# A second MLP's weights: 64-bit words made into floats early and kept in DRAM

## The chip, the cores and the metric

The kernel runs on one core of a Trainium2 chip. The metric is device time in microseconds (us). The kernel before took 886.29 us (median of 3 runs, 883.88 to 888.55).

## The reference, cut to what matters

Attention over four batches of eight heads of 576 x 64 (a local band plus a four-fold downsampled attention) gives `x`, four batches of 576 x 512. Then a first block with a LayerNorm and an MLP, and a second block with a token MLP and a channel MLP:

```
x  = x + relu(LN(x) * g_ln @ moe_w_ch1) @ moe_w_ch2          # 512 -> 2048 -> 512
h  = relu(x^T @ w_tok1) @ w_tok2                             # over the 576 tokens, 576 -> 256 -> 576
u  = x + h^T
out = u + relu(u @ w_ch1) @ w_ch2                            # 512 -> 1536 -> 512
```

The weights come as 64-bit floats; the attention inputs and the result are 32-bit.

## The kernel before, in words

**Numbers.** A product of 32-bit floats is made of three TensorE passes over a high and a low part (`PASSES`: high by high, high by low, low by high). So each operand exists as `hi` (a rounded copy) and `lo` (the rest). Weights are read as pairs of 32-bit integers. `convert_steps` makes a 32-bit float `f` of each pair with three VectorE operations (exponent, sign, tail; L257, L262, L267), then ScalarE copies `f` to `hi` (L272) and VectorE subtracts to get `lo` (L275). The raw words lie in a staging slot (tag `st`), `f` in a buffer of the tag `cv`, `hi` and `lo` in a weight buffer of the pool `wp`.

**Units and chunks.** The 2304 tokens are 18 tiles of 128, and two tiles make a chunk: nine chunks for each MLP (0 to 8 for the first, 9 to 17 for the second). A unit is 128 of the hidden columns in one chunk. The first MLP has 16 units a chunk (`UA`), the second 12 (`UB`). For unit `i` of the sequence the first product `g1` (L875, 12 matmuls of 256 columns), `relu` on ScalarE (L884), `low` on VectorE (L888) and the second product `g2` (L901, 6 matmuls of 512 columns) follow each other, and `g1` of unit `i + 1` is put before `g2` of unit `i`. The accumulators leave at the end of a chunk (`evac`, L910 and L914). Units 0 to 111 (chunks 0 to 6) stand in a written order together with the attention (`STEPS`). From unit 112 on a loop emits the steps, and `put(position, step)` hangs other work on a unit: `put(131.5, ...)` comes after the second product of unit 131, a whole number before it.

**What sets the order.** A planner takes the emitted steps as priorities and places each instruction on its engine as early as its own simulated times, its inputs and a free buffer allow. Work that was put on unit 113 can so run beside units of a lower number, between the written steps. `keep_in_program_order` pins one instruction behind the one emitted before it on its engine. Each engine then runs its list in order, and all loads and stores are issued by SyncE's queue (SP), in order too.

**The weights.** A unit's weights are two pieces of 512 x 128 words (`NPC` = 2): the first piece is for `g1`, the second for `g2`. `wp` has 16 buffers, and in chunks 7 and 8 all of them hold units of the first MLP. So a unit of the second MLP gets a buffer only when chunk 8 (units 128 to 143) has used a unit for the last time. The token MLP's relu results take buffers of the same pool. When the attention is over, `close_att` opens a new staging pool with two `st` slots and two `cv` buffers; the token weights (`load_tok`, 9 pieces) and the second MLP's 24 pieces use it. `units_b` adds the 24 pieces to a list at unit 129, `w_load` issues as many loads as there are slots, and `w_split` (one call for each unit, from unit 131.5 on, one unit apart) converts two pieces and loads the next ones:

```
    for m in range(UB):
        put(bw + 3.5 + m, w_split, NPC)
```

**Beside it** stand the token steps (`put_tok`): `xs_load` (L968, L970) into one buffer `xr`, `xs_split` (ScalarE L976, GpSimd L977), `tok1` (TensorE L992), `tok_relu`, and for each chunk `u_load` (L1009), `tok2` (L1023, L1028) and the turning of the chunk's tokens (`xt_turn`: 16 transfers of 16 KB for each tile on SP, L818, then L830 and L835).

Of the kernel before, what the change touches and what calls it, by code (L numbers as in the profile page):

```python
# [7 lines left out]
F32 = mybir.dt.float32  # L8
F32R = mybir.dt.float32r
I32 = mybir.dt.int32  # L10
ACTF = mybir.ActivationFunctionType
ALU = mybir.AluOpType
# [4 lines left out]
DM = H * D  # L17
# [19 lines left out]
QW = 512  # L37
# [160 lines left out]
def block_kernel(ctx: ExitStack, tc: tile.TileContext, qk, vw, vh, vg, g_ln, wa, t1, t2, wb, band, near, lv, edge, out):  # L198
    nc = tc.nc
    UA = wa.shape[0]  # L200
    UB = wb.shape[0]
# [3 lines left out]
    dram = ctx.enter_context(tc.tile_pool(name="dram", bufs=1, space=DRAM))  # L205
    wp = ctx.enter_context(tc.tile_pool(name="wp", bufs=UA))
# [7 lines left out]
    att_ctx = ExitStack()  # L214
    at = att_ctx.enter_context(tc.tile_pool(name="at", bufs=1))
    sp_ctx = ExitStack()
    sp = {"pool": sp_ctx.enter_context(tc.tile_pool(name="sp", bufs=1)), "n": 3}

    up_scr = [dram.tile([S, 128], F32, name=f"up_scr{n}") for n in range(B * NP)]
    loc_scr = {n: dram.tile([2 * NTL * QB, 128], F32, name=f"loc_scr{n}") for n in range(NP, B * NP)}  # L220
    x2_scr = [dram.tile([128, CT, DM], F32, name=f"x2_scr{c}") for c in range(NCH)]

    ident = const.tile([128, 128], F32, name="ident")
# [15 lines left out]
    def f32(ap):  # L239
        return ap.bitcast(F32)  # L240
# [3 lines left out]
    wt = {}  # L244

    wa, wb, t1, t2 = (w.bitcast(I32) for w in (wa, wb, t1, t2))

    def stage(n):
        return sp["pool"].tile([128, 2 * QW], I32, tag="st", name="st", bufs=sp["n"])[:, :2 * n]

    def convert_steps(raw, hi, lo, n):
        r = raw.rearrange("p (n t) -> p n t", t=2)
        h, l = r[:, :, 1], r[:, :, 0]
        f = sp["pool"].tile([128, QW], I32, tag="cv", name="cv", bufs=2)[:, :n]

        def exponent():
            return nc.vector.tensor_scalar(  # L257
                out=f, in0=h, scalar1=3, scalar2=0x3FFFFFFF, op0=ALU.logical_shift_left, op1=ALU.bitwise_and
            )

        def sign():
            nc.vector.scalar_tensor_tensor(  # L262
                out=f, in0=h, scalar=-0x40000000, in1=f, op0=ALU.bitwise_and, op1=ALU.bitwise_or
            )

        def tail():
            nc.vector.scalar_tensor_tensor(  # L267
                out=f, in0=l, scalar=29, in1=f, op0=ALU.logical_shift_right, op1=ALU.bitwise_or
            )

        def split_hi():
            nc.scalar.activation(out=hi, in_=f.bitcast(F32), func=ACTF.Copy)  # L272

        def split_lo():
            nc.vector.tensor_tensor(out=lo, in0=f.bitcast(F32), in1=f32(hi), op=ALU.subtract)  # L275

        return [exponent, sign, tail, split_hi, split_lo]

    def convert(raw, hi, lo, n):
        for f in convert_steps(raw, hi, lo, n):  # L280
            f()

    ld_w = {}
    NPC = 2 * DM // QW

    def load_unit(i, part, gate=None):
        w, m = (wa, i) if i < UA else (wb, i - UA)
        if i < EARLY:
            if part == 0:
                t = wp.tile([128, NPC, 2 * QW], I32, tag="w", name="raw")  # L290
                for k in range(NPC):
                    ld_w[i, k] = t[:, k]
            raw = ld_w[i, part]
        else:
            raw = ld_w[i, part] = stage(QW)
        if gate is not None:
            nc.vector.tensor_copy(raw[:, 0:1].bitcast(F32), gate)
        nc.sync.dma_start(out=raw, in_=w[m, part])

    def split_steps(i, part):  # L300
        if part == 0:
            wt[i] = wp.tile([128, 2, 2, DM], F32R, tag="w", name="w")
        t = wt[i]
        e, o = divmod(part * QW, DM)
        return convert_steps(ld_w.pop((i, part)), t[:, e, 0, o:o + QW], t[:, e, 1, o:o + QW], QW)
# [732 lines left out]
    def put(pos, f, *args):  # L1038
        u, half = divmod(int(2 * max(pos, UNITS)), 2)
        u = min(u, NSEQ - 1)  # L1040
        (bg if half else mid)[u].append(lambda: f(*args))
# [24 lines left out]
    pieces = [(i, part) for i in range(UA) for part in range(NPC)]  # L1066
    nl, nsp = [0], [0]

    def w_load(n):
        while n and nl[0] < len(pieces) and nl[0] - nsp[0] < sp["n"]:  # L1070
            load_unit(*pieces[nl[0]])
            nl[0] += 1
            n -= 1
# [103 lines left out]
    def close_att():  # L1177
        vec_ctx.close()
        att_ctx.close()
        sp["n"] = 2  # L1180
        sp["pool"] = ctx.enter_context(tc.tile_pool(name="sp2", bufs=1))
        tok["pool"] = ctx.enter_context(tc.tile_pool(name="tok", bufs=1))

    bt = base[NCH - 2]
    put(base[NCH - 1] - 5, rota.__setitem__, slice(None), ["g"])
    put(bt, close_att)
    for i in range(NTL + 4):
        put(bt + 1 + i, load_tok, i)
    put_tok(0, base[NCH - 1] - 4)
    put_tok(1, base[NCH - 1] + 3)  # L1190

    def units_b():
        pieces.extend((UA + i, part) for i in range(UB) for part in range(NPC))

    bw = base[NCH - 1]
    put(bw + 1, units_b)
    put(bw + 1, lambda: w_load(sp["n"]))
    for m in range(UB):
        put(bw + 3.5 + m, w_split, NPC)
    for c in range(NCH, 2 * NCH):  # L1200
        put_prep2(c, base[c] - 1)
    put_tok(2, base[NCH + 2])
# [133 lines left out]
```

## Time and profile before

| | us |
|---|---|
| median of 3 runs | 886.29 (883.88 to 888.55) |
| the profiled execution | 886.56 |
| its span, first to last instruction | 884.8 |
| TensorE matmuls busy (PE) | 863.8 (98%) |
| TensorE weight loads busy (PEld) | 766.3 (87%) |
| VectorE (DVE) | 518.4 (59%) |
| ScalarE (ACT) | 251.4 (28%) |
| GpSimd (POOL) | 193.6 (22%) |
| SP's transfers, share of the 16 DMA engines | 39.4% |

Times in the trace count from the first instruction of the span. A busy time is the sum of the instructions on that engine. PE's weight loads overlap its matmuls. The chain of waits is followed back from the last instruction to what released it; by engine PE has 66% of it, VectorE 19%, transfers 8%.

### The profile page before, as it was taken

The page shows a single profiled execution, that of the slowest core. Times are in us where ns is not written, and L with a number is a line of the kernel's source. Part 1 is how long each engine was busy: PE and PEld are TensorE (multiplying, and loading weights), DVE is VectorE, ACT ScalarE, POOL GpSimd, SP SyncE. Part 2 cuts the span into 40 slices and gives each one's busy share as a digit, 9 for nine tenths or more (in the row PEclk, how much of TensorE's full clock was granted, in tenths as well). Part 3 has the DMA queues.
Part 4 walks back from the last instruction along what each step waited for, and adds up shares of the span by engine and source line. Part 5 has one row for each costly group of instructions (what it writes and reads, how often), then busy time and mean ns, then how long its engine had stood idle before and what let it go on. Part 6 is the DMA issues. An engine that isn't in the chain of part 4 may idle for free.

```text
span 884.8 us, 16767 instructions
## 1 busy us (share of the span) xinstructions
PE 863.8 (98%) x6418; PEld 766.3 (87%) x6418; DVE 518.4 (59%) x1114; ACT 251.4 (28%) x713; POOL 193.6 (22%) x197
## 2 busy tenths in 40 slices
PE   7999999999999999999999999989999999999998
PEld 6888899887989999989999887879898898999997
DVE  5999999999998776832222779863213232222221
ACT  5665535354322111322111233222121111111111
POOL 7731323566873510111000000110010000000000
PEclk9999999999999999999999999999999999999999
DMA  9747776578662522532111356632222121121100
GB/s 280 193 151 225 225 237 199 148 199 224 168 150 72 139 49 60 175 92 89 36 37 48 107 155 178 193 115 53 52 56 46 29 67 35 17 45 23 31 24 24
DMA packets 126752, 98.39 MB, mean 111 GB/s; under 512 B 78744, under 2 KB 104376, under 8 KB 126672
## 3 DMA queue, kind: packets, MB, share of 16 engines
q1 hardware_dynamic: 126672, 97.31, 39.4%
q8 instruction: 51, 0.84, 0.4%
q14 instruction: 29, 0.24, 0.1%
HBM read 72.87 MB, written 16.53 MB: 101 GB/s over the span
## 4 chain that ended last, share of the span: by engine, by line
PE 66%; DVE 19%; DMA 8%; SPq 3%; issue 2%; POOL 1%; ACT 1%; DVEq 0%; ACTq 0%; POOLq 0%
PE h L875 30%; PE acc L901 27%; DMA xr<-x_scr 3%; DMA st<-in_wb_dram 3%; SPq L818 3%; PE k L901 2%; DVE cv L267 2%; PE g L1023 2%; DVE ht L888 1%; DVE cv L262 1%; DVE lp L718 1%; DVE la L726 1%; DVE cv L257 1%; PE k L992 1%; DMA up_scr<-od 1%
## 5 line engine op out<-in xcount | busy, mean ns | idle before, releaser
L875 PEld LDWEIGHTS h<-xt,w 128*128 128x128 f32 x3024 | 394.2, 191 | 22.9 <-DVE ht L888 2.1
L875 PE MATMUL h<-xt,w 128*128 128x256 f32 x3024 | 404.8, 284 | 1.4 <-DVE ht L888 1.3
L901 PE MATMUL acc<-w,ht 128*128 128x512 f32 x1416 | 367.7, 395 | 3.0 <-DVE ht L888 2.4
L901 PEld LDWEIGHTS acc<-w,ht 128*128 128x128 f32 x1416 | 253.5, 189 | 52.3 <-DVE ht L888 4.6
L888 DVE SCALAR_TENSOR_TENSOR ht<-h,ht 128x256 fp32r<-128x256 f32 x252 | 105.6, 419 | 273.4 <-ACT ht L884 273.0
L884 ACT ACTIVATE ht<-h 128x256 fp32r<-128x256 f32 x252 | 96.7, 384 | 439.0 <-PE h L875 355.8
L977 POOL TENSOR_TENSOR xs<-xr,xs 128x512 fp32r<-128x512 f32 x20 | 26.5, 1323 | 293.3 <-ACT xs L976 293.3
L272 ACT ACTIVATE w<-cv 128x512 fp32r<-128x512 f32 x56 | 35.5, 635 | 66.6 <-DVE cv L267 66.5
L684 POOL TENSOR_TENSOR lp<-lqk 128x576 f32<-128x576 f32 x28 | 40.4, 1444 | 43.2 <-DVE ls L690 31.5
L275 DVE TENSOR_TENSOR w<-cv,w 128x512 fp32r<-128x512 f32 x56 | 42.8, 767 | 4.3 <-ACT w L272 4.1
L267 DVE SCALAR_TENSOR_TENSOR cv<-st,cv 128x512 int32<-128x512 int32 (+4 forms) x63 | 44.2, 703 | 0.4
L655 POOL TENSOR_TENSOR x<-x,et 128x256 f32<-128x256 f32 (+2 forms) x40 | 32.0, 820 | 50.6 <-DMA et<-loc_scr 40.0
L262 DVE SCALAR_TENSOR_TENSOR cv<-st,cv 128x512 int32<-128x512 int32 (+4 forms) x63 | 41.5, 659 | 0.4
L257 DVE TENSOR_SCALAR cv<-st 128x512 int32<-128x512 int32 (+4 forms) x63 | 27.3, 433 | 15.2 <-DMA st<-in_wb_dram 10.5
L455 POOL TENSOR_TENSOR vg<-vg 72x256 f32<-72x256 f32 x39 | 31.4, 806 | 18.3 <-DMA vg<-in_vg_dram 15.3
L992 PE MATMUL k<-xs,t1w 128*128 128x512 f32 (+1 forms) x120 | 32.1, 406 | 2.6 <-ACT xs L976 1.9
L1023 PE MATMUL g<-r,t2w 128*128 128x512 f32 x120 | 34.0, 394 | 0.0
L830 ACT ACTIVATE xt<-xt 128x512 fp32r<-128x512 f32 x30 | 18.9, 631 | 34.6 <-DMA xt<-xc 31.2
L835 DVE TENSOR_TENSOR xt<-xt 128x512 fp32r<-128x512 f32 x30 | 24.1, 803 | 7.3 <-ACT xt L830 7.0
L901 PE MATMUL k<-w,ht 128*128 128x512 f32 x96 | 26.0, 403 | 0.1
L992 PEld LDWEIGHTS k<-xs,t1w 128*128 128x128 f32 (+1 forms) x120 | 19.2, 188 | 7.9 <-ACT xs L976 2.8
L1023 PEld LDWEIGHTS g<-r,t2w 128*128 128x128 f32 x120 | 20.9, 189 | 3.0
(189 smaller groups left out, 656.4 us busy)
## 6 DMA issues: line engine op xcount, KB each, us to landing
st<-in_wa_dram SPq DMA_DIRECT2D x28, 512.0 KB
st<-in_wb_dram SPq DMA_DIRECT2D x24, 512.0 KB
xt<-xc SPq DMA_DIRECT2D x480, 16.0 KB
qk<-in_qk_dram SPq DMA_DIRECT2D x13, 581.0 KB
x_scr<-x SPq DMA_DIRECT2D x18, 256.0 KB
x<-x_scr SPq DMA_DIRECT2D x9, 512.0 KB
out_dram<-x SPq DMA_DIRECT2D x18, 256.0 KB
xr<-x_scr SPq DMA_DIRECT2D x16, 256.0 KB
```

Source lines behind the costliest of these rows:

```text
L257: return nc.vector.tensor_scalar(out=f, in0=h, scalar1=3, scalar2=0x3FFFFFFF, op0=ALU.logical_shift_left, op1=ALU.bitwise_and)
L262: nc.vector.scalar_tensor_tensor(out=f, in0=h, scalar=-0x40000000, in1=f, op0=ALU.bitwise_and, op1=ALU.bitwise_or)
L267: nc.vector.scalar_tensor_tensor(out=f, in0=l, scalar=29, in1=f, op0=ALU.logical_shift_right, op1=ALU.bitwise_or)
L272: nc.scalar.activation(out=hi, in_=f.bitcast(F32), func=ACTF.Copy)
L275: nc.vector.tensor_tensor(out=lo, in0=f.bitcast(F32), in1=f32(hi), op=ALU.subtract)
L684: nc.gpsimd.tensor_tensor(out=t["pr"], in0=t["qk"][:, :VQ], in1=t["qk"][:, VQ + D * o:VQ + D * o + VQ], op=ALU.mult)
L875: nc.tensor.matmul(out=hp[:, :CN], lhsT=w[:, 0, a, kk * 128:(kk + 1) * 128], rhs=xT[c][:, kk, e, :], start=(n == 0), stop=(n == 3 * KD - 1),)
L884: nc.scalar.activation(out=t[:, 0], in_=hps[i][:, :CN], func=ACTF.Relu)
L888: nc.vector.scalar_tensor_tensor(out=t[:, 1], in0=hp[:, :CN], scalar=0.0, in1=f32(t[:, 0]), op0=ALU.max, op1=ALU.subtract)
L901: nc.tensor.matmul(out=acc[c, j], lhsT=t[:, a, j * 128:(j + 1) * 128], rhs=w[:, 1, e, :], start=(m == 0 and n == 0), stop=(last and n == 2),)
L992: nc.tensor.matmul(out=rps[b, m], lhsT=tokw["t1"][rows, a, n, m * 128:(m + 1) * 128], rhs=t[rows, e, :], start=(n == 0 and i == 0), stop=( ...
L1023: nc.tensor.matmul(out=ps, lhsT=tokw["t2"][:, a, m, o:o + 128], rhs=r_t[b][:, m, e, :], start=(i == 0), stop=(i == len(ops) - 1),)
```

## The change

All 24 pieces of the second MLP's weights are converted to 32-bit floats by the three integer operations, put from unit 115 on at 0.85 units apart, and each is written from its `cv` buffer to a DRAM tensor `w_scr[m]`. From unit 130 on, one unit at a time is read back as floats (one load of 512 KB into one staging slot, which so holds both pieces), and from unit 131.5 on `b_split` makes `hi` on ScalarE and `lo` on VectorE in a weight buffer. The pinned instruction of a unit was VectorE's first integer operation of each piece; it is now ScalarE's first copy of each unit. The number of slots and of `cv` buffers stays two each.

```diff
+    w_scr = [dram.tile([128, 2 * DM], F32, name=f"w_scr{m}") for m in range(UB)]
...
-    def convert_steps(raw, hi, lo, n):
+    def convert_steps(raw, hi, lo, n, f=None):
...
-        f = sp["pool"].tile([128, QW], I32, tag="cv", name="cv", bufs=2)[:, :n]
+        if f is None:
+            f = sp["pool"].tile([128, QW], I32, tag="cv", name="cv", bufs=sp["cv"])[:, :n]
...
-    def units_b():
-        pieces.extend((UA + i, part) for i in range(UB) for part in range(NPC))
+    def pre_load(k):
+        if k < UB * NPC:
+            t = ld_w["b", k] = stage(QW)
+            nc.sync.dma_start(out=t, in_=wb[k // NPC, k % NPC])
+
+    def pre_f32(k):
+        m, part = divmod(k, NPC)
+        raw = ld_w.pop(("b", k))
+        f = sp["pool"].tile([128, QW], I32, tag="cv", name="cv", bufs=sp["cv"])
+        for step in convert_steps(raw, None, None, QW, f)[:3]:
+            step()
+        nc.sync.dma_start(out=w_scr[m][:, part * QW:(part + 1) * QW], in_=f.bitcast(F32))
+
+    def b_load(m):
+        if m < UB:
+            t = ld_w["f", m] = stage(QW).bitcast(F32)
+            nc.sync.dma_start(out=t, in_=w_scr[m])
+
+    def b_split(m):
+        t, w = ld_w.pop(("f", m)), wp.tile([128, 2, 2, DM], F32R, tag="w", name="w")
+        wt[UA + m] = w
+        for part in range(NPC):
+            e, o = divmod(part * QW, DM)
+            f, hi, lo = t[:, part * QW:(part + 1) * QW], w[:, e, 0, o:o + QW], w[:, e, 1, o:o + QW]
+            ins = nc.scalar.activation(out=hi, in_=f, func=ACTF.Copy)
+            if part == 0:
+                tc.keep_in_program_order(ins)
+            nc.vector.tensor_tensor(out=lo, in0=f, in1=f32(hi), op=ALU.subtract)
 
     bw = base[NCH - 1]
-    put(bw + 1, units_b)
-    put(bw + 1, lambda: w_load(sp["n"]))
+    put(bt + 2, pre_load, 0)
+    for k in range(UB * NPC):
+        put(bt + 3 + 0.85 * k, pre_load, k + 1)
+        put(bt + 3 + 0.85 * k, pre_f32, k)
+    put(bw + 2, b_load, 0)
     for m in range(UB):
-        put(bw + 3.5 + m, w_split, NPC)
+        put(bw + 3 + m, b_load, m + 1)
+        put(bw + 3.5 + m, b_split, m)
```

Here `bt` is unit 112 and `bw` unit 128.

## Rows read from the trace of the kernel before

**Rows 1.** Busy time (and count) of each engine by stretch, clock, DMA share, GB/s.

```profile
core 0: us, PE busy (x) PEld busy (x) DVE busy (x) ACT busy (x) POOL busy (x), PEclk, DMA share, GB/s
340.00:480.00 140.00, 139.54 (x881) 125.42 (x880) 57.26 (x154) 28.98 (x71) 9.05 (x7) 1.00 0.28 77
480.00:530.00 50.00, 50.00 (x292) 44.06 (x291) 34.80 (x73) 13.73 (x28) 2.57 (x2) 1.00 0.43 123
530.00:600.00 70.00, 65.70 (x372) 54.12 (x371) 54.84 (x94) 21.10 (x45) 9.67 (x7) 1.00 0.53 159
```

**Rows 2.** The same view, for line 875 (first product) alone: PE, then PEld.

```profile
530.00:600.00 70.00, 27.67 (x200) 26.23 (x198) 1.00 0.53 159
744.00:814.00 70.00, 39.38 (x300) 38.66 (x299) 1.00 0.16 32
```

**Rows 3.** The same, for line 901 (second product).

```profile
530.00:600.00 70.00, 27.20 (x96) 16.80 (x96) 1.00 0.53 159
744.00:814.00 70.00, 37.94 (x149) 26.71 (x150) 1.00 0.16 32
```

**Rows 4.** The same, for line 992 (first token product).

```profile
530.00:600.00 70.00, 9.19 (x36) 5.23 (x36) 1.00 0.53 159
```

**Rows 5.** The same, for line 1023 (second token product).

```profile
530.00:600.00 70.00, 11.09 (x40) 7.13 (x41) 1.00 0.53 159
```

**Rows 6.** The chain that ended last, by time: start, us, what.

```profile
565.02 6.83 DMA st<-in_wb_dram
575.80 4.20 DMA xr<-x_scr
...
780.61 2.87 PE h L875 x24
783.49 2.75 PE acc L901 x12
```

**Rows 7.** Timeline of TensorE: start, us, instructions, [idle before, its releaser].

```profile
535.78 1.21 PE L901 MATMUL acc<-w,ht 128*128 128x512 f32 x4 [0.59 <-ACT ht L884]
...
580.79 0.73 PE L992 MATMUL k<-xs,t1w 128*128 128x512 f32 x2 [1.61 <-ACT xs L976]
...
587.89 0.97 PE L992 MATMUL k<-xs,t1w 64*128 64x512 f32 x6
```

**Rows 8.** Timeline of VectorE: end of chunk 8, the last low halves of weights.

```profile
541.10 1.40 DVE L910 SCALAR_TENSOR_TENSOR x<-acc,y,x 128x512 f32<-128x512 f32 x2
...
587.06 1.37 DVE L275 TENSOR_TENSOR w<-cv,w 128x512 fp32r<-128x512 f32 x1 [0.96 <-ACT w L272]
```

**Rows 9.** By stretch, for line 275 (low halves) alone: VectorE busy, count.

```profile
480.00:530.00 50.00, 6.14 (x9) 1.00 0.43 123
530.00:600.00 70.00, 12.29 (x15) 1.00 0.53 159
```

**Rows 10.** Groups by line, 440 to 620 us: busy, mean ns, idle before and releasers.

```profile
L888 DVE SCALAR_TENSOR_TENSOR ht<-h,ht 128x256 fp32r<-128x256 f32 x51 | 21.4, 420 | 51.6 <-ACT ht L884 51.6
...
L884 ACT ACTIVATE ht<-h 128x256 fp32r<-128x256 f32 x50 | 18.9, 378 | 60.0 <-PE h L875 52.8 <-PE acc L901 6.9 <-PE g L1023 0.3
...
L267 DVE SCALAR_TENSOR_TENSOR cv<-st,cv 128x512 int32<-128x512 int32 x24 | 18.0, 749 | 0.2
L262 DVE SCALAR_TENSOR_TENSOR cv<-st,cv 128x512 int32<-128x512 int32 x24 | 17.0, 709 | 0.2
...
L272 ACT ACTIVATE w<-cv 128x512 fp32r<-128x512 f32 x24 | 15.2, 632 | 49.4 <-DVE cv L267 49.4
...
L257 DVE TENSOR_SCALAR cv<-st 128x512 int32<-128x512 int32 x24 | 10.5, 438 | 10.6 <-DMA st<-in_wb_dram 10.5
```

**Rows 11.** Waits of SP's queue, 440 to 612 us: total, times, longest us.

```profile
SPq L298 <- DVE cv L267: 17.2, 13, 4.2
```

**Rows 12.** Waits of VectorE, 440 to 620 us.

```profile
DVE cv L257 <- DMA st<-in_wb_dram: 10.5, 9, 2.2
```

**Rows 13.** Timeline of SP's queue: issue of a weight load, transposes, two stores.

```profile
376.49 0.33 SPq L298 DMA_DIRECT2D st<-in_wb_dram  x1
...
378.88 10.32 SPq L818 DMA_DIRECT2D xt<-xc  x16
...
541.99 1.01 SPq L919 DMA_DIRECT2D x_scr<-x  x2
```

More of the change, by code (lines that the diff above doesn't have):

```diff
@@ L216, in block_kernel @@
     sp_ctx = ExitStack()
-    sp = {"pool": sp_ctx.enter_context(tc.tile_pool(name="sp", bufs=1)), "n": 3}
+    sp = {"pool": sp_ctx.enter_context(tc.tile_pool(name="sp", bufs=1)), "n": 3, "cv": 2}
     up_scr = [dram.tile([S, 128], F32, name=f"up_scr{n}") for n in range(B * NP)]
     loc_scr = {n: dram.tile([2 * NTL * QB, 128], F32, name=f"loc_scr{n}") for n in range(NP, B * NP)}
+    w_scr = [dram.tile([128, 2 * DM], F32, name=f"w_scr{m}") for m in range(UB)]
     x2_scr = [dram.tile([128, CT, DM], F32, name=f"x2_scr{c}") for c in range(NCH)]
@@ L1179, in close_att @@
         att_ctx.close()
-        sp["n"] = 2
+        sp["n"], sp["cv"] = 2, 2
         sp["pool"] = ctx.enter_context(tc.tile_pool(name="sp2", bufs=1))
```

## The prediction

> **What bounds the kernel now.** I read the page first, then a table by stretch, then the chain of waits, and last the timelines of single engines. By the page TensorE is busy for 98% of the span, so the change can only be worth time in which TensorE does not issue at its own pace. The table by stretch shows where that is [rows 1]: from 480 to 530 us TensorE is busy for all 50.00 us, from 340 to 480 for 139.54 of 140, but from 530 to 600 for only 65.70 of 70. The granted clock is 1.00 in all three, so it is not the clock.
>
> Busy time understates the loss, because a matmul that starts late still counts as busy while it drains. I count matmuls instead. In a dense stretch of the chain 24 matmuls of 256 columns take 2.87 us, 0.1196 us each, and 12 of 512 columns take 2.75 us, 0.229 us each [rows 6]. Tested on 744 to 814 us: 300 x 0.1196 + 149 x 0.229 = 70.0 us of 70 [rows 2, 3]. From 530 to 600 there are 200 of the first kind, 96 + 40 of the second, and 36 of the first token product [rows 2 to 5]. Twelve of these 36 use 64 rows, and six such took 0.97 us, 0.16 us each [rows 7]. So 23.9 + 22.0 + 9.2 + 24 x 0.229 + 12 x 0.16 = 62.5 us of work in 70 us: **7.5 us lost**. That is the pool; the dense stretch shows none, and I take the rest after 600 us to be like it.
>
> The Trainium skill (Perfetto Trace Analysis, Identifying the Most-Contended Engine) says that a busy matmul row is a poor measure of headroom and that busy weight loads are a better one. By the first, the pool is 4.3 us; by the second, weight loads fall from 88% (480 to 530) to 77% (530 to 600) [rows 1], an estimate of (0.881 - 0.773) x 70 / 0.881 = 8.6 us. The count agrees with the second.
>
> What holds TensorE there? The stretch is the end of chunk 8 (its accumulators leave at 541.1 us [rows 8]) and chunk 9, the first that uses the second MLP's units. Of the 24 pieces of its weights, 15 get their low half only after 530 us [rows 9], the last at 587.06, and behind a 0.96 us wait [rows 8]. The pieces come late because only two staging slots take the 64-bit words. A slot is held from the issue of its load until the last of three integer operations. The load queue waited 17.2 us for exactly that release [rows 11], VectorE waited 10.5 us for the loads [rows 12], and one load lay 6.83 us on the chain [rows 6]. The SP queue is in order, so the token stage's loads of `xr` stand behind those waiting loads: a 4.20 us `xr` load on the chain at 575.80 [rows 6], then the 1.61 us TensorE gap on ScalarE's `xs` at 580.79 [rows 7]. The gap of 0.59 us at 535.78 ends with a relu that stood behind a weight copy on ScalarE [rows 7].
>
> **The change, part by part.**
>
> *Moved: three integer operations of 24 pieces.* One piece costs 0.438 + 0.709 + 0.749 = 1.90 us [rows 10], 45.5 us in all. They no longer need a `wp` buffer, so nothing ties them to units that chunk 8 must finish first; they need a staging slot and a `cv` buffer. Before the change the first such load was issued at 376.49 [rows 13], and its slot was then held until chunk 8 freed a weight buffer. So the stage is open from about 375 us and the moved work will fill 375 to 460. VectorE is busy there for 57.26 of 140 us [rows 1]; with 45.5 more it is 73%. That is the density of 480 to 530 (34.80 of 50, 70%), which held nine conversions and no TensorE gap [rows 1, 9]. The cover is that `low` may be late: behind a unit's first product stand 1.4 us of the previous unit's second product and 1.4 us of the next first product, less 0.38 us of relu and 0.42 us of `low` [rows 10], so some 2 us of slack, more than any one of the moved operations. If the cover is gone, each microsecond in excess is lost. Bounds: nothing (480 to 530), or, by the far row, as in 530 to 600: 7.5 us over 15 pieces, 0.5 us a piece, 12 us. The near one is the idle time of 340 to 480, 0.46 us [rows 1], beside the token weights' conversions. I take 0.6 us.
>
> *Added: 24 writes of 256 KB, and 12 reads of 512 KB in place of 24.* On SP a store costs 0.5 us to issue and a load 0.33 [rows 13]: 24 x 0.83 = 20 us between 375 and 460, where two chunks' transposes take some 41 us (two to a chunk, 16 issues in 10.32 us [rows 13]). SP stays below its time. Queued behind a write that waits for `cv` are transposes, `xr` loads and stores, all used tens of microseconds later: I cost it at nothing. A `cv` buffer is free only when its write has landed, and VectorE's next first operation waits for that, with `low` behind it; this is inside the 0 to 12 us above.
>
> *Left in place: the high copy and the low subtraction.* 24 of each, ScalarE's 0.63 us [rows 10] and VectorE's 12.29 / 15 = 0.82 us [rows 9], 35 us over two engines, from unit 131 on. The pinned instruction is now on ScalarE and waits for the read; relus stand behind it. Before, the pinned one was on VectorE with `low` behind it, and waits of up to 2.2 us [rows 12] fitted the slack.
>
> *Are the units in time?* By the order of the statements two float reads take both slots before the last three pieces are converted, so about 13 more slot uses follow the first split. At 4.2 to 6.83 us a load [rows 6] and 1.4 us of splitting, two slots need 13 x 5.6 / 2 = 36 to 13 x 8.2 / 2 = 53 us. The first split stands 12 units before 541 us, at 2.81 us a unit at least, no later than 507: done by 543 to 560. The last unit is wanted 11 units after 541, at 572. So they are in time, and chunk 9 no longer waits.
>
> *What is late next?* The `xr` chain: one buffer, a load, 0.63 us, a GpSimd subtraction, and again. With no stalled weight load before it on SP it needs no more than it has. I leave 1.4 us of the 7.5 for the copies that still stand before relus near 535 and for such token waits.
>
> **Sum**, against the profiled execution (886.56 us, a span of 884.8 and 1.8 around it, 0.3 above the median of the runs): 7.5 - 1.4 recovered, 0.6 added, so 886.56 - 5.5 = **881.0 us**.
>
> **Rivals.**
> A. *The units stay just in time.* If ScalarE's pinned copies wait for reads that are behind 16 transposes on SP (10.32 us), the weights come late again, or the token chain keeps its gaps. For it: the same two slots, one queue. Against: half the loads and a third of the slot time. Half of the loss stays: 886.56 - 3.1 = 883.5.
> B. *The moved work stops TensorE where it did not stop before* (the other side). Place: 375 to 460 us, VectorE waiting for a load or for a write to free `cv`, `low` behind it. It outweighs the 6.1 us recovered from 6.1 / 24 = 0.25 us a piece. At 0.5 us, as in 530 to 600, it costs 12 us: 886.56 + 5.9 = 892.5. Against: the nine pieces before 530 cost nothing.
> C. *It doesn't do what it says*: the planner, which pulls work ahead by its own times, puts the conversions where they were, or moves token products into new gaps of the same size. Time: 886.5. Against: the load of 376.49 shows that the planner goes ahead as soon as a slot is free.
>
> **How the numbers follow.** Forecast 0.62, with a range of its own of 878.5 to 883.5; A 0.17; B 0.10; C 0.11. The end 878.5 is all of the 7.5 us and a little of the 0.46 us. Up to 886.5 takes in A and nearly all of C; B's upper part is left out. A measurement here can tell 0.5%, 4.4 us, from no change: faster means below 881.9. That holds most of the forecast's chance (0.53 of 0.62) and 0.01 of A; slower (above 890.7) is the larger part of B, 0.07; 0.39 is left for the same.
>
> **What would show it.** Right: the 24 first integer operations lie between about 370 and 460 us; from 530 to 600 TensorE's busy time is above 69 of 70; SP's wait of a weight load for the integer operation is gone from that stretch; the last low subtraction ends before 570 us; from 340 to 480 TensorE stays above 139. Wrong: TensorE gaps behind `ht` in 375 to 460 (B), ScalarE's copies waiting for float reads with relus behind them (A), or gaps of the same sum moved past 600 us (C).

## The result, and the profile after

The changed kernel takes 896.79 us (median of 4, 893.33 to 899.35) against 885.86 us for the kernel before on the same chip (4 runs). The ratio is 1.0116 [1.0093, 1.0140]: some 10 us slower, where 5.5 us faster had been forecast. The profiled execution took 893.33 us (span 891.5), 6.8 us more than that of before, and was the fastest of its four.

The table by stretch of the kernel after (its columns are those of [rows 1]):

```profile
340.00:480.00 140.00, 136.46 (x848) 120.78 (x847) 78.34 (x186) 27.99 (x70) 9.41 (x7) 1.00 0.47 141
480.00:530.00 50.00, 45.91 (x271) 40.08 (x270) 35.12 (x74) 10.79 (x24) 1.29 (x1) 1.00 0.79 235
530.00:600.00 70.00, 67.82 (x394) 58.85 (x393) 30.98 (x56) 22.83 (x47) 7.74 (x6) 0.98 0.43 123
744.00:814.00 70.00, 70.00 (x436) 63.05 (x435) 20.93 (x40) 10.63 (x26) 0.00 (x0) 1.00 0.15 31
```

TensorE gained 2 us of busy time from 530 to 600, and lost 3 us from 340 to 480 and 4 us from 480 to 530, two stretches that were whole before [rows 1]. The late stretch, 744 to 814, is whole in both.

The same view for the first product alone (now L877), then for the second (L903):

```profile
380.00:500.00 120.00, 61.68 (x467) 60.35 (x468) 1.00 0.53 162
500.00:530.00 30.00, 10.85 (x84) 10.70 (x83) 1.00 0.75 211
530.00:600.00 70.00, 29.89 (x222) 28.94 (x220) 0.98 0.43 123
```

```profile
380.00:500.00 120.00, 59.02 (x230) 40.57 (x228) 1.00 0.53 162
500.00:530.00 30.00, 11.35 (x42) 7.64 (x42) 1.00 0.75 211
530.00:600.00 70.00, 30.40 (x113) 20.75 (x114) 0.98 0.43 123
```

With the prices of the prediction (0.1196 and 0.229 us a matmul, 0.16 for the first token product's 64-row ones) and the token products of each stretch (24, 30 and 59 of them), the count gives what each stretch lost. From 380 to 500, for example: 467 x 0.1196 + 230 x 0.229 + 18 x 0.229 + 6 x 0.16 = 113.6 of 120, so 6.4 us lost.

| us lost | 380-500 | 500-530 | 530-600 | 600-640 | sum |
|---|---|---|---|---|---|
| before | 1.1 | -0.1 | 7.5 | -0.2 | 8.3 |
| after | 6.4 | 3.5 | 4.5 | 1.3 | 15.7 |
| difference | +5.3 | +3.6 | -3.0 | +1.5 | +7.4 |

Instructions cut by an edge and missing records make each entry uncertain by about 1 us. The sum of the differences, 7.4 us, answers to the 6.8 us between the two profiled executions. The Trainium skill (Perfetto Trace Analysis, Identifying the Most-Contended Engine) holds busy weight loads a better measure than busy matmuls. The four products' weight loads in 380 to 500 fell from 109.6 to 104.7 us, an estimate of 5.4 us of the 120; the count's 5.3 agrees.

The larger gaps of TensorE from 380 to 600 us after (timeline; in brackets the idle time before the group and what ended it):

```profile
415.89 1.70 PE L877 MATMUL h<-xt,w 128*128 128x256 f32 x12 [0.61 <-DVE ht L890]
423.32 1.65 PE L903 MATMUL acc<-w,ht 128*128 128x512 f32 x6 [1.53 <-ACT ht L886]
...
436.88 1.70 PE L877 MATMUL h<-xt,w 128*128 128x256 f32 x12 [0.96 <-DVE ht L890]
483.19 1.70 PE L877 MATMUL h<-xt,w 128*128 128x256 f32 x12 [0.96 <-DVE ht L890]
514.65 1.65 PE L903 MATMUL acc<-w,ht 128*128 128x512 f32 x6 [1.77 <-ACT ht L886]
523.28 0.98 PE L903 MATMUL acc<-w,ht 128*128 128x512 f32 x3 [1.37 <-DVE ht L890]
560.30 1.75 PE L903 MATMUL acc<-w,ht 128*128 128x512 f32 x4 [2.13 <-ACT ht L886]
```

Every one ends with `ht`: a relu (ScalarE, L886) or its low part (VectorE, L890) came late, never a weight as such. The token gap of 1.61 us at 580.79 [rows 7] is gone. What stood before those `ht` is in the timelines of the two engines. VectorE:

```profile
421.73 0.38 DVE L259 TENSOR_SCALAR cv<-st 128x224 int32<-128x224 int32 x2 [5.20 <-DMA st<-in_t_dram]
...
436.06 0.43 DVE L259 TENSOR_SCALAR cv<-st 128x512 int32<-128x512 int32 x1 [2.82 <-DMA st<-in_wb_dram]
436.40 0.42 DVE L890 SCALAR_TENSOR_TENSOR ht<-h,ht 128x256 fp32r<-128x256 f32 x1
```

VectorE stood 2.82 us at an integer operation whose load had not landed; the next instruction in its list is the `low` that TensorE's group at 436.88 waited for. Not every `low` stood behind a wait alone: those of the gaps at 415.89 and 483.19 had all three integer operations (of token weights, of a piece) between the wait (2.52 and 1.09 us) and themselves. ScalarE, around the gaps of 514.65 and 560.30:

```profile
513.17 1.15 ACT L1218 ACTIVATE w<-st 128x512 fp32r<-128x512 f32 x2 [5.69 <-DMA st<-w_scr]
514.23 0.64 ACT L886 ACTIVATE ht<-h 128x256 fp32r<-128x256 f32 x2
...
556.28 1.16 ACT L1218 ACTIVATE w<-st 128x512 fp32r<-128x512 f32 x2 [6.97 <-DMA st<-w_scr]
```

ScalarE stood 5.69 us at a high copy whose float read was on its way, with two relus behind it. The waits of the whole second part (us in total, times, longest):

```profile
ACT w L1218 <- DMA st<-w_scr: 29.2, 11, 7.0
...
DVE cv L259 <- DMA st<-in_wb_dram: 17.4, 13, 2.8
DVE cv L259 <- DMA st<-in_t_dram: 16.3, 7, 5.2
...
DVE cv L259 <- DMA w_scr<-cv: 3.6, 2, 2.1
```

Before, VectorE waited 10.5 us for the second MLP's loads [rows 12] and 4.5 us for the token weights'; now the waits for the three kinds of loads are 62.9 us on two engines. The `cv` buffers are a small part of it.

The loads and reads by line (issue times in ns; first and last start in us):

```profile
L1197 SPq DMA_DIRECT2D st<-in_wb_dram x24: 328/380/590, 360.2 to 524.6; - x24
L1210 SPq DMA_DIRECT2D st<-w_scr x12: 325/427/691, 501.9 to 560.7; - x12
L947 SPq DMA_DIRECT2D st<-in_t_dram x5: 367/432/517, 354.6 to 399.7; - x5
L952 SPq DMA_DIRECT2D st<-in_t_dram x4: 423/423/430, 408.2 to 457.9; - x4
```

The 24 pieces' loads run from 360 to 525 us. The nine token weights, which before had all been issued by 374.8, now share the two slots with them until 458, and the float reads share them until 525. The chain of waits has one such slot in turn:

```profile
469.16 4.78 DMA st<-in_wb_dram
474.50 0.70 DVE cv L264
475.23 0.69 DVE cv L269
476.31 4.59 DMA st<-in_wb_dram
```

From load to load 7.15 us pass, 4.6 to 4.8 of them in the transfer; with two slots a piece takes 3.6 us. So two thirds of a round are transfer, and VectorE's 1.9 us are the smaller part.

Last, the gap of 560.30 was followed by a lower granted clock (columns as in [rows 1]):

```profile
560.00:562.00 2.00, 1.70 (x5) 1.37 (x6) 1.61 (x4) 0.24 (x1) 0.00 (x0) 0.68 0.80 260
562.00:564.00 2.00, 2.00 (x7) 1.52 (x6) 0.61 (x2) 1.28 (x3) 0.00 (x0) 0.50 0.70 195
564.00:566.00 2.00, 2.00 (x13) 1.78 (x12) 1.02 (x3) 0.73 (x3) 0.00 (x0) 0.97 0.53 127
```

0.50 is the lower of the two levels, 1.2 GHz. Going by these rows (0.32 + 0.50 + 0.03) x 2 = 1.7 us of the 4.5 us lost in 530 to 600 are clock, at most, since TensorE stood idle for the first 0.3 us of them.

### The profile page after: what moved, and what is told of

It reads as the page before. It is cut to its first block, busy times and chain, and to the rows that moved or that the text cites. A ratio compares the mean times of both kernels' runs of the same rounds, so it can differ in the third digit from the quotient of the medians.

```text
span 891.5 us, 16838 instructions
## 1 busy us (share of the span) xinstructions
PE 865.7 (97%) x6418; PEld 766.4 (86%) x6418; DVE 516.9 (58%) x1114; ACT 250.8 (28%) x713; POOL 196.7 (22%) x197
## 4 chain that ended last, share of the span: by engine, by line
PE 66%; DVE 17%; DMA 8%; SPq 5%; issue 2%; ACT 1%; POOL 0%; DVEq 0%; ACTq 0%
PE h L877 29%; PE acc L903 26%; DMA st<-in_wb_dram 4%; SPq L820 4%; DMA st<-in_t_dram 2%; PE k L903 2%; PE g L1025 2%; PE k L994 2%; DVE cv L269 2%; DVE cv L264 2%; DVE ht L890 2%; DVE cv L259 1%; DVE lp L720 1%; DVE la L728 1%; DVE ls L692 1%
## 5 line engine op out<-in xcount | busy, mean ns | idle before, releaser
L877 PEld LDWEIGHTS h<-xt,w 128*128 128x128 f32 x3024 | 393.8, 191 | 24.0 <-DVE ht L890 3.9
L877 PE MATMUL h<-xt,w 128*128 128x256 f32 x3024 | 404.1, 283 | 2.5 <-DVE ht L890 2.5
L903 PE MATMUL acc<-w,ht 128*128 128x512 f32 x1416 | 369.2, 395 | 9.0 <-ACT ht L886 5.8
L903 PEld LDWEIGHTS acc<-w,ht 128*128 128x128 f32 x1416 | 254.1, 189 | 60.8 <-ACT ht L886 7.1
L890 DVE SCALAR_TENSOR_TENSOR ht<-h,ht 128x256 fp32r<-128x256 f32 x252 | 105.5, 419 | 245.0 <-ACT ht L886 244.5
L886 ACT ACTIVATE ht<-h 128x256 fp32r<-128x256 f32 x252 | 96.3, 384 | 455.0 <-PE h L877 390.3
L457 POOL TENSOR_TENSOR vg<-vg 72x256 f32<-72x256 f32 x39 | 34.2, 878 | 19.6 <-DMA vg<-in_vg_dram 17.4
L994 PE MATMUL k<-xs,t1w 128*128 128x512 f32 (+1 forms) x120 | 34.5, 410 | 0.1
L837 DVE TENSOR_TENSOR xt<-xt 128x512 fp32r<-128x512 f32 x30 | 21.6, 719 | 12.8 <-ACT xt L832 12.7
L903 PE MATMUL k<-w,ht 128*128 128x512 f32 x96 | 25.8, 403 | 0.0
L274 ACT ACTIVATE w<-cv 128x512 fp32r<-128x512 f32 x32 | 20.4, 636 | 18.2 <-DVE cv L269 17.9
L1221 DVE TENSOR_TENSOR w<-st,w 128x512 fp32r<-128x512 f32 x24 | 16.5, 714 | 14.6 <-ACT w L1218 14.5
L277 DVE TENSOR_TENSOR w<-cv,w 128x512 fp32r<-128x512 f32 x32 | 23.2, 729 | 0.1
```

The costliest lines, as they stand in the source:

```text
L457: nc.gpsimd.tensor_tensor(out=vd[:, :, :, :D], in0=vd[:, :, :, :D], in1=vgt[:, :, o:o + 128].rearrange("p c (h d) -> p c h d", h=2), op=AL ...
L877: nc.tensor.matmul(out=hp[:, :CN], lhsT=w[:, 0, a, kk * 128:(kk + 1) * 128], rhs=xT[c][:, kk, e, :], start=(n == 0), stop=(n == 3 * KD - 1),)
L886: nc.scalar.activation(out=t[:, 0], in_=hps[i][:, :CN], func=ACTF.Relu)
L890: nc.vector.scalar_tensor_tensor(out=t[:, 1], in0=hp[:, :CN], scalar=0.0, in1=f32(t[:, 0]), op0=ALU.max, op1=ALU.subtract)
L903: nc.tensor.matmul(out=acc[c, j], lhsT=t[:, a, j * 128:(j + 1) * 128], rhs=w[:, 1, e, :], start=(m == 0 and n == 0), stop=(last and n == 2),)
L994: nc.tensor.matmul(out=rps[b, m], lhsT=tokw["t1"][rows, a, n, m * 128:(m + 1) * 128], rhs=t[rows, e, :], start=(n == 0 and i == 0), stop=( ...
```

## The experiments

Two theories. **An engine stands at a transfer**: the moved integer operations wait on VectorE for loads, `low` behind them (the early loss; V in the expectations), and ScalarE's copies wait for reads, relus behind them (the late loss; R). A variant of the early part is S (start): it comes of the token weights' loads in the same two slots. The rival, on which the forecast rested: **the integer work itself** and its place are what TensorE waits for, so that taking it out of 530 to 600 gives its time back. The time of each run is told as a ratio to the kernel before on the same chip; us lost are counted as above, from one profiled execution each, which in some kernels is not a middling one (said where it matters).

| | ratio to before | 380-500 | 500-530 | 530-600 | 600-640 |
|---|---|---|---|---|---|
| after, again (e5) | 1.0118 [1.0079, 1.0157] | 6.6 | 3.9 | 5.0 | 1.0 |
| e1 late | 1.0046 [1.0024, 1.0069] | 6.7 | 0.3 | 2.4 | 1.3 |
| e2 no pin | 1.0087 [1.0060, 1.0114] | 6.8 | 3.2 | 2.2 | 1.2 |
| e3 direct | 1.0087 [1.0057, 1.0118] | 5.0 | -0.2 | 6.0 | 0.0 |
| e4 no integer work | 1.0010 [0.9979, 1.0041] | 0.8 | -0.3 | 7.7 | -0.2 |
| e6 early part alone | 1.0338 [1.0289, 1.0386] | 6.5 | 2.0 | 20.6 | 8.6 |
| e7 late, direct, far | 1.0099 [1.0064, 1.0134] | 5.4 | -0.3 | 4.8 | 0.8 |
| e8 as e4, half loads | 0.9985 [0.9963, 1.0007] | 0.9 | -0.1 | 3.2 | 1.0 |
| e9 as e1, half loads | 1.0042 [1.0009, 1.0075] | 7.5 | 0.1 | 4.0 | 0.5 |
| e10 spread and pinned | 1.0000 [0.9987, 1.0013] | 2.3 | 0.3 | 6.5 | 0.6 |
| e11 e10 without its pin | 1.0065 [1.0040, 1.0090] | 6.9 | -0.4 | 8.2 | 0.9 |
| e12 as e10, copies later | 1.0087 [1.0059, 1.0115] | 2.0 | -0.3 | 10.8 | 0.5 |

**e1: the early conversions put behind the token weights.**

```diff
-    put(bt + 2, pre_load, 0)
+    put(bt + 9.5, pre_load, 0)
     for k in range(UB * NPC):
-        put(bt + 3 + 0.85 * k, pre_load, k + 1)
-        put(bt + 3 + 0.85 * k, pre_f32, k)
+        put(bt + 9.5 + 0.4 * k, pre_load, k + 1)
+        put(bt + 9.5 + 0.4 * k, pre_f32, k)
```

> The early conversion is put behind the token weights (first load at unit 121.5, pieces 0.4 units apart), nothing else differs from the changed kernel. Theory S (start): sharing the two slots with the token weights costs the 4.7 us lost between 400 and 440 us; then TensorE is gap-free there and the time falls from about 897 to 892. Theory R (reads): the loss is ScalarE standing at the float reads with relus behind it after 500 us; then the time stays within 2 us of 897, or rises, since the conversion ends no earlier.

889.56 us (median of 10; the profiled execution, 893.02, was the slowest). The time fell as S had it, but not where S had it. All token weights are issued by 379 us and the last piece's load at 502.3 (524.6 after), so the reads no longer share the slots with pieces. Of the 8.0 us lost from 500 to 600, 2.7 are left. The early loss stays, with VectorE's waits for the pieces' loads (23.2 us, 19 times, 340 to 620). So the mixing of three kinds of transfers in two slots cost the larger part of the late loss. Without it the early loss is as large as with it, now behind the pieces' loads alone.

**e2: no pin on ScalarE's copy.**

```diff
-            if part == 0:
-                tc.keep_in_program_order(ins)
```

> The changed kernel without the pin on ScalarE's first copy of a unit. If the pin itself holds ScalarE (part of theory R): ScalarE's waits for float reads fall well below the 29 us of the changed kernel and the time goes to about 892. If the copies stand where they do because the planner takes the reads as landed sooner than they land, the waits and the time stay (895 to 899). Theory S: no change, 897.

892.89 us (median of 5). ScalarE still waits 27.0 us, 10 times, for the reads: the planner of itself places the copies where their reads have not landed. The time, though, is nearer to the 892 that was expected if the pin held ScalarE. With 1.0087 left the pin is not the whole cause; a part of it, 2 to 3 us by the middle values, is neither shown nor ruled out, as the intervals overlap (1.0060 to 1.0114 here, 1.0093 to 1.0140 for the kernel after).

**e3: floats read straight into the low half of a weight buffer, the copy two units later.**

```diff
-            t = ld_w["f", m] = stage(QW).bitcast(F32)
-            nc.sync.dma_start(out=t, in_=w_scr[m])
+            w = wt[UA + m] = wp.tile([128, 2, 2, DM], F32R, tag="w", name="w")
+            nc.sync.dma_start(out=f32(w[:, :, 1]), in_=w_scr[m].rearrange("p (e n) -> p e n", e=2))
...
+        put(bw + 2.5 + 2 + m, b_split, m)
```

> The floats are read straight into the low half of the weight buffer (no staging slot), copied to the high half two units later and subtracted in place. Theory R: ScalarE no longer waits for reads (under 8 us in all from 29), the gaps after 500 us go, 4 to 6 us: 891 to 893. Theory S: the 4.7 us between 400 and 440 us stay, and so does most of the time above 890.

893.62 us (median of 5). The waits of ScalarE's copies were not under 8 us but 24.2 us. The loss of 500 to 530 is gone, but a gap of 2.25 us behind a relu stands at 555.43, and 6.0 us are lost from 530 to 600. Slots for the reads were part of it, not the whole.

**e4: the kernel before without the second MLP's three integer operations** (the high words taken as floats).

```diff
+        f = raw.rearrange("p (n t) -> p n t", t=2)[:, :, 1].bitcast(F32)
+        return [
+            lambda: nc.scalar.activation(out=hi, in_=f, func=ACTF.Copy),
+            lambda: nc.vector.tensor_tensor(out=lo, in0=f, in1=f32(hi), op=ALU.subtract),
+        ]
```

> The kernel before, with the three integer operations of the second MLP's pieces left out (the high word of each pair is used as it is, so the weights are not the reference's). It asks what the moved work was worth at most. If the three operations and the slot time they hold are what stops TensorE from 530 to 600 us: 6 us less than before, 880. If it is the loads themselves and the token chain: 2 us or less, 884 to 886.

The decisive miss for the forecast. With all 45.5 us of the moved work taken out, and nothing added, the time is the same: 886.4 us, 1.0010 [0.9979, 1.0041]. The waits of e4 (340 to 620 us; its L311 is the high copy, L892 the relu):

```profile
ACT w L311 <- DMA st<-in_wb_dram: 32.4, 22, 3.7
...
PE acc L909 <- ACT ht L892: 4.8, 4, 2.0
```

and the two largest of its four gaps of TensorE in 530 to 600:

```profile
560.47 1.65 PE L909 MATMUL acc<-w,ht 128*128 128x512 f32 x6 [1.36 <-ACT ht L892]
...
572.57 2.07 PE L909 MATMUL acc<-w,ht 128*128 128x512 f32 x4 [2.03 <-ACT ht L892]
```

VectorE's wait for the load became ScalarE's, with relus behind it: without the integer operations the first instruction of a piece, the pinned one, is ScalarE's copy. The token gap of 1.61 us [rows 7] is gone, and all four gaps are now behind relus. So taking the integer work out gained nothing, because loads still landed after an in-order engine had come to them. It does not show that the integer operations had no part in the pool of the kernel before: the loss is of the same size (7.7 against 7.5 us) but made of other gaps. No run left the operations out without putting the pin before the relus. (The profiled execution of e4 took 892.3 us, above its median: its trace shows the mechanism, the ratio the size.)

**e5: the changed kernel again**, beside e6 to e8.

> The changed kernel again, to stand beside the others on one chip. All theories: 893 to 899.

897.28 us (median of 4): the same loss in the same stretches, with a gap of 2.79 us behind a relu at 518.71 in this execution.

**e6: the kernel before, with the early conversion and the writes added** and the floats not used (pieces 0.6 units apart).

```diff
+    put(bt + 2, pre_load, 0)
+    for k in range(UB * NPC):
+        put(bt + 3 + 0.6 * k, pre_load, k + 1)
+        put(bt + 3 + 0.6 * k, pre_f32, k)
     put(bw + 1, units_b)
```

> The kernel before, its second MLP made as before, with the early conversion added and its floats never read (24 loads, the integer operations, 24 writes; pieces 0.6 units apart, so that they end before the old path begins). Theory V (VectorE stands at loads in the early stretch, low behind it): 4 to 8 us more than before, 889 to 893, with gaps between 380 and 500 us. If the early part is covered, as the prediction had it: 885 to 887.

916.75 us (median of 4), far above both expectations. Up to 500 us it loses 6.5 us, as the kernel after does: the early loss comes from the early conversion with its writes, and no read has a part in it. Past 500 it tells nothing on the change, because the old path's loads then start at 518.4 us instead of 376.5, and all of chunk 9 is late.

**e7: e1 and e3 together, the copies five units after the reads.**

```diff
+        put(bt + 9.5 + 0.4 * k, pre_load, k + 1)
...
+        put(bw + 2.5 + 5 + m, b_split, m)
```

> The changed kernel with the early conversion behind the token weights, the floats read straight into the weight buffer, and their copies five units after the read. Theory R (an engine that works in order stands at a load that lands later than the planner took it to, relu behind it): ScalarE's waits for the float reads fall from 20 to 29 us to under 8, the gaps behind relu after 500 us go, and what is left is the early stretch: 885 to 888. If the distance does not matter: as the one with the late start, 889 to 890.

895.57 us (median of 5; the profiled execution, 890.37, was the fastest), not 885 to 888. ScalarE's waits fell to 16.7 us, but one read took 9.16 us to land (issued at 542.58) and 4.9 us were lost in 530 to 600. Distance in units alone did not bring the reads in before their copies.

**e8: e4 with half of each load** (half of the words read, each used twice).

```diff
+            nc.sync.dma_start(out=raw[:, :QW], in_=w[m, part][:, :QW])
```

> The kernel before without the three integer operations and with half of each load (256 KB in place of 512 KB, each value used twice, so the weights are not the reference's); the same copies and subtractions. If the time that a load needs to land is what stops TensorE from 530 to 600 us (theory R): 880 to 882, and ScalarE's waits for these loads fall from 32 us to under 15. If it is the number of waits or the token chain: as without the operations alone, 885 to 887.

885.08 us (median of 10). The same two waits as in e4 (L317, L898):

```profile
ACT w L317 <- DMA st<-in_wb_dram: 20.5, 14, 3.7
...
PE acc L915 <- ACT ht L898: 1.7, 3, 0.8
```

With loads of 256 KB the waits shrink by a third, TensorE's by two thirds, and the loss of 530 to 600 goes from 7.7 to 3.2 us. The ratio to before, 0.9985 [0.9963, 1.0007], still takes in no change at all, so even this bound, half the bytes and none of the integer work, is worth at most 3.3 us of the 7.5. That is the expectation's second branch (885 to 887), not the 880 to 882 of the landing time alone. The pin stands on ScalarE's copy here too.

**e9: e1 with half of each early load.**

```diff
-            nc.sync.dma_start(out=t, in_=wb[k // NPC, k % NPC])
+            nc.sync.dma_start(out=t[:, :QW], in_=wb[k // NPC, k % NPC][:, :QW])
```

> The early conversion behind the token weights (as in the run with the late start), with half of each of its loads (256 KB, each pair used twice, so the weights are not the reference's) and the same three operations. Landing time decides: VectorE's waits for these loads fall from 23 us to under 8, and of the 5 us lost between 380 and 500 us under 2 are left; time 885 to 887. If the operations themselves or SP's queue cost it: the loss stays at 4 to 6 us and the time at 889 to 890.

891.73 us (median of 7). VectorE's waits fell only from 23.2 to 17.2 us and the early loss stayed (7.5 us). So the transfer's size is not what sets the early loss: with shorter loads VectorE came to them early all the same, and the pieces' loads were issued over 113.5 us in place of 121.6. The loss is on the side of the expectation's second branch, the operations themselves or SP's queue; the run does not tell these from waits that cost something wherever they fall. What it suggested was the planner, which places each operation where it expects the load to have landed.

**e10: pieces 1.25 units apart, the first integer operation pinned**, token weights first, direct reads as in e3. **e11: the same without the pin on the integer operation** (without the second hunk).

```diff
-        put(bt + 1 + i, load_tok, i)
+        put(bt + 0.5, load_tok, i)
...
-        for step in convert_steps(raw, None, None, QW, f)[:3]:
+        first, *rest = convert_steps(raw, None, None, QW, f)[:3]
+        tc.keep_in_program_order(first())
+        for step in rest:
             step()
...
+        put(bt + 1 + 1.25 * k, pre_load, k + 1)
+        at_m = max(bw + 2.5 + m, bt + 3.5 + 2.5 * m)
+        put(at_m, b_load, m)
+        put(at_m + 4, b_split, m)
```

> Everything of the change is kept, with more time for each transfer: token weights first, early pieces 1.25 units apart and their first operation pinned to that place, floats read straight into the weight buffer four units before the copies. If standing at late transfers is the whole cause: TensorE loses under 3 us after 340 us (7 before the change, 14 with it), time 880 to 883, below the kernel before. If the added transfers or SP's queue cost something of their own: 886 to 892.

> As the one with spread pieces, without the pins on the integer operations. If the planner moves them ahead to the time at which it takes the loads as landed: VectorE waits for the loads again (15 us or more), gaps before 500 us come back, 3 to 6 us over the pinned one. If the distance in the list is enough: as the pinned one within 1 us.

e10: 887.74 us (median of 12), no different from before and not the 880 to 883 that was expected if standing at late transfers were the whole cause; what the added transfers and SP's queue cost stays unmeasured. e11: 894.22 us (median of 7). Both profiled executions (889.63 and 896.36) are at the upper end of their runs. The table by stretch of e10:

```profile
380.00:530.00 150.00, 148.98 (x913) 131.89 (x912) 76.58 (x169) 29.79 (x70) 6.59 (x5) 1.00 0.52 159
```

and of e11:

```profile
380.00:530.00 150.00, 145.19 (x890) 128.03 (x889) 83.47 (x181) 28.60 (x67) 6.50 (x5) 1.00 0.58 180
```

One pin is worth 23 matmuls in 150 us. Without it the planner drew the operations ahead of their place: the last piece's load is issued at 501.4 us, with the pin at 547.5. VectorE's waits are fewer with the pin (17.0 us, 10 times, against 23.7 and 17), but what counts is what stands behind one. In e10:

```profile
455.64 0.43 DVE L259 TENSOR_SCALAR cv<-st 128x512 int32<-128x512 int32 x1 [3.33 <-DMA st<-in_wb_dram]
```

and TensorE has no gap between 380 and 475 us. Up to 438 us nothing was there to stop it: e10 converts no piece before 438.1 us, and five only after 530, while e11 has begun eleven by 440. The same count of matmuls, cut at 440 us, shows how much the place decides:

| us | after | e1 | e9 | e11 | e10 |
|---|---|---|---|---|---|
| lost, 380-440 | 5.0 | 5.0 | 6.0 | 4.2 | 0.2 |
| lost, 440-500 | 1.2 | 1.3 | 1.0 | 2.5 | 1.6 |
| VectorE's waits for pieces' loads, 380-440 | 2.8 | 10.3 | 8.8 | 12.0 | 0 |
| the same, 440-500 | 10.2 | 12.1 | 8.4 | 11.7 | 15.6 |

(In the kernel after, 11.0 us of waits for token weights come on top in 380-440.) Beside waits of much the same length TensorE loses 4 to 6 us before 440 and 1 to 2.5 us after it. TensorE's order differs there. In the kernel before:

```profile
421.09 2.91 PE L901 MATMUL acc<-w,ht 128*128 128x512 f32 x12
...
450.64 1.55 PE L901 MATMUL acc<-w,ht 128*128 128x512 f32 x6
```

Up to some 437 us many second products come in twos, so the `low` of the second unit is covered by only one second product, 1.4 us less 0.8 us of relu and `low`, 0.6 us in place of 2. No run changed that order, so that it is the reason is argued, from these rows.

What e10 keeps is the late loss, 6.5 us; the largest gap of its TensorE timeline:

```profile
570.43 1.19 PE L903 MATMUL acc<-w,ht 128*128 128x512 f32 x4 [2.17 <-ACT ht L886]
```

It ends with a relu behind a copy that waits for a read (29.6 us in 12 waits in all), though the reads are emitted four units ahead.

**e12: e10 with pieces 1.1 units apart and the copies seven units after the reads.**

```diff
+        at_m = max(bw + 2.5 + m, bt + 3.5 + 2.2 * m)
+        put(at_m, b_load, m)
+        put(at_m + 7, b_split, m)
```

> As the run with spread and pinned pieces, with the pieces 1.1 units apart, so that the last floats are written earlier, and ScalarE's copies seven units after the read in place of four. If what is left after 530 us is still ScalarE standing at a read with relu behind it: its waits for the reads fall from 30 us to under 10, the loss of 530 to 600 us from 6 to under 3 us, time 882 to 885, below the kernel before. If the end is set by something else (the transposes of the next chunk, the token chain): as the run with spread pieces, ratio 0.998 to 1.002.

891.99 us (median of 6), a miss. The late loss changed its form: SP issued three reads and two loads of 512 KB between 522.1 and 525.4 us, and a load of `xr` right behind them. On e12's chain:

```profile
526.79 8.12 DMA xr<-x_scr
```

and on TensorE, with the table by stretch after it:

```profile
535.70 0.80 PE L994 MATMUL k<-xs,t1w 64*128 64x512 f32 x2 [4.24 <-ACT xs L978]
```

```profile
530.00:532.00 2.00, 1.46 (x7) 0.88 (x5) 1.76 (x5) 1.15 (x2) 0.00 (x0) 1.00 1.03 408
532.00:534.00 2.00, 0.00 (x0) 0.00 (x0) 2.00 (x5) 0.00 (x0) 0.00 (x0) 1.00 1.11 278
...
538.00:540.00 2.00, 1.32 (x4) 0.50 (x2) 1.32 (x3) 1.60 (x3) 0.00 (x0) 0.50 0.48 149
540.00:542.00 2.00, 2.00 (x9) 1.84 (x9) 1.52 (x3) 0.01 (x1) 0.00 (x0) 0.50 0.90 282
```

An `xr` load took 2.7 to 2.8 us on the chain of the kernel after, and 8.12 here, where the DMA engines are full (share 1.03 and 1.11). TensorE stood 4.24 us and then ran at the lower clock. That transfers of any issuing engine share the same 16 DMA engines and interleave there is said by the Trainium skill (DMA: Bandwidth & Descriptors, Issuing engines are not separate DMA queues); the 8.12 us agree with it as far as SP's own transfers go, and no run here issues loads from another engine. Bringing the reads forward collided with the token stage's loads.

No version beat the kernel before; e10 equals it.

## Why the prediction was wrong

**The pool: right in size, wrong in what would free it.** 7.5 us were lost in 530 to 600 and the wait of weight loads for the integer operation was there [rows 11, 12]. But e4 took the integer operations away and the time stayed the same. The step from this pool to "7.5 - 1.4 recovered" by moving the integer operations failed: it should have been asked who takes the weights next, and whether they will have landed by then. In e4 ScalarE waited for the same loads (32.4 us).

**Moved work at 0.6 us: this step failed.** It measured 5.3 us, 0.22 us a piece (e6 has it alone). The argument was by busy share (73% against 70% in 480 to 530) and by `low` having 2 us of slack. The 73% spread the work over 140 us, though it was to fill 85: from 375 to 460 VectorE was busy for 25.26 us before, so 45.5 more would have been 83%. VectorE's busy share was in fact lower than estimated, 78.34 of 140 us, 56%, since part of the moved work came later; TensorE lost time all the same, as waits of 2 to 5 us for a load do not show in a busy share and exceed the slack. The slack itself, some 2 us, holds only where first and second products alternate; most of the early loss (5.0 of 6.4 us) came before 440 us, where many second products come in twos and it is 0.6 us by the same reckoning. And the nearest row, nine conversions without a gap in 480 to 530, was of operations whose first one was pinned. The change moved that pin to ScalarE, the planner drew the freed operations ahead, and e10 against e11 shows what the pin was worth early on, above all by keeping the operations out of 380 to 440. That the planner does so because it expects a load to land sooner than it does is argued, from e9; no run shows its times.

**Rival B happened, below its own threshold.** Its place, VectorE at loads with `low` behind, is the one measured. At 0.22 us a piece, under the 0.25 from which it was to decide, it would only have used up the 6.1 us to be recovered.

**Recover 6.1 of 7.5: failed too.** 530 to 600 gave back 3.0 us, and 3.6 and 1.5 us were lost before and after it. This is rival A, ScalarE's copies waiting for reads (29.2 us) with relus behind, at a higher price than A's half of the pool. e1 shows that the larger part came from pieces still in the slots beside the reads. The prediction had seen that the last pieces follow the first reads, and had counted slot times for it, but not the engine that waits meanwhile. Its sum with the measured terms: 886.56 + 5.3 + 3.6 - 3.0 + 1.5 = 894.0, against 893.33. Each rival had been priced alone with all else going well; the range so ended at 886.5, and with both at once the kernel took 897.

**Place and duration: failed.** The pieces' first integer operations lie from 371.4 to 528.6 us, not 370 to 460: the token weights share the slots, and the `put` positions of the last pieces lie behind the first reads. Two slots at 7.15 us a round are 86 us for the 24 pieces alone, a reckoning that had been made only for the reads.

**Units in time by 543 to 560: nearly.** The last copy is at 566.0 and the last low subtraction at 567.3 us, inside the 572 that the last unit allows and the 570 named as a sign. But arriving in time for the last unit did not help the units whose relus stood behind the copies.

**Writes at nothing: not settled.** The waits of SP's own queue after:

```profile
SPq L1205 <- DVE ht L890: 22.7, 11, 3.6
SPq L1197 <- DMA st<-in_t_dram: 17.9, 7, 4.8
SPq L1197 <- DVE cv L269: 17.0, 8, 3.4
```

The queue stood at the writes (L1205) for 22.7 us in that row alone. As the next load mostly needs the same conversion's end, this may cost nothing; no run had the conversions without the writes.

**Right:** the token gap of 580.79 went, as did SP's wait of weight loads for the integer operation from 530 us on; the writes' `cv` buffers cost little (3.6 us of waits); and the count of matmuls closed on the measured difference.

**Still open:** why the copies wait for reads that are emitted four to seven units ahead (e7, e10, e12), whether for full DMA engines or for the planner's placing of the copies; what the integer operations were worth in the pool of the kernel before; whether the early loss follows from the order of the second products; and how much of the excess in the medians over the profiled executions (10.3 against 6.8 us) is the lower clock, which depends on where a gap falls.

## What to carry to other kernels

Idle time of an in-order engine hides an operation only if its data have landed when the engine comes to it; otherwise the price is what stands behind the wait, and a busy share doesn't show it. A slack reckoned from one order of instructions holds only where that order holds. Before moving suspected work, run the kernel without it, and look whether the old gaps are gone or others have come in their place: here that one run gained nothing. Where a planner orders the work, a pin that goes away is part of the change and has a price of its own.

## What the runs showed of the hardware

- Of eight gaps of TensorE between 2.0 and 2.8 us (340 to 760 us of all traces), seven were followed by a granted clock at or near 0.50 for some 2 to 4 us (2.13 in the kernel after, 2.03 in e4, 2.79 and 2.26 in e5, 2.48 in e6, 2.17 in e10, 2.41 in e11); e3's of 2.25 us was not. The gap of 4.24 us (e12) was followed by 0.50 from 536 to 544. Gaps of up to 1.95 us left 1.00 (e7, 558 us; [rows 7] for 1.61). In the kernel after it cost up to 1.7 us, beside the gap's 2.13.
- A 512 KB load into a slot took 3.2 to 4.8 us on the chain when two were under way; with several in flight a read took 9.16 us (e7) and a load of `xr` 8.12 us (e12).
